# A spectral filter and a gated FFN on one core: four excursions per batch moved to other steps, their output buffers to another pool, and the last block's copies to VectorE

## The chip, the core and the metric

The kernel runs on one core of a Trainium2 chip. The metric is the device time of one execution in microseconds (us). Times inside an execution come from one profiled execution, counted from the start of its span. Engines: PE is TensorE (PEld its weight loads), DVE is VectorE, ACT is ScalarE, POOL is GpSimd, SP is SyncE, which here issues nearly all DMAs.

## The reference

The input x is 8 x 3008 x 256 (batch, sequence, channel). Along the sequence each channel is multiplied in the frequency domain by a filter; the result, as 24064 tokens of 256 channels, goes through a gated FFN with 1536 hidden units.

```python
X = np.fft.rfft(x, axis=1)
Y = X * (filt_r + 1j * filt_i)[None]
y = np.fft.irfft(Y, n=3008, axis=1).reshape(24064, 256)
out = (np.maximum(y @ w_gate, 0) * (y @ w_val)) @ w_out
```

## The kernel before

The sequence length is split as 3008 = 94 x 32, and the transform is done in stages by matmuls. For a batch b:

- **Stage A** (transforms of length 94) reads x and writes the buffer Abuf[b] in device memory.
- **Stage B** reads it back into the tile `at`, does the transforms of length 32, multiplies by the filter and transforms back; it writes Dbuf[b]. It has 14 items (`items_b`), most with two psX matmuls, two multiplications on DVE, four psD matmuls and a copy on ACT (dsb). Four of the items end with a store to Dbuf.
- **Stage C** (`item_c`) reads Dbuf[b] back into dC tiles and forms one half of the FFN's input tile yT, 512 tokens wide.
- **The FFN** goes over 47 blocks of 512 tokens. A block has 12 steps. In each step `gv` does four matmuls (psV, psG) for 128 hidden units, ACT copies psV to vsb and DVE forms prod from psG and vsb; `o_part` does four psO matmuls of the block before. At steps 5 and 11 of a block, psO is copied to osb and stored to the output. Steps are numbered through: step s is step s mod 12 of block s // 12.

Batch 0, and batch 1's stage A, are done in a prologue in a form of their own (`items_a`), in which ACT copies to the tile `asb` and SP stores it to Abuf. The other stages are woven into the FFN's steps: a table `side` says which functions are called at which step, after that step's gv and o_part. The engines work in the order in which the program was written, each with its own queue; semaphores connect them. Nothing is rescheduled.

For batches 2 to 7 stage A is done in four chunks j. Three calls belong to a chunk:

- `load_chunk`: six DMAs on SP from x to the tile XP[j % 2]. There are two such tiles, so chunk 2 uses that of chunk 0 again, and chunk 3 that of chunk 1.
- `fold_chunk`: six additions and subtractions on POOL, in XP and a second tile, `fold`.
- `tiled_a`, the excursion: 16 matmuls in the source (32 records in the trace) on quarters of the array, 24 rows by 32 columns, from XP and `fold` to four PSUM tiles psF; four copies to bf16 in the tile `asf`, two on ACT and two on DVE; four DMAs on SP from asf to Abuf.

Then `load_at_tiled` reads Abuf back with eight DMAs. The first item of stage B stands at step sb0: 93, 165, 237, 309, 381 and 453 for batches 2 to 7. The items stand at sb0, sb0 + 2, ..., sb0 + 26, all odd steps; batch 1's begin at 19. At sb0 + 27 `load_d` asks SP for the eight reads of Dbuf. [...]

Memory on the chip comes from pools. `sb` lasts for the whole kernel, `pro` is closed after the prologue, and `fs` is opened then, in the memory that pro had. A tile of fs has to wait for whatever still uses the tiles of pro that were there. Before the change asb lies in pro, and asf in fs.

In the last block `o_part` runs alone after all gv; its four copies are on ACT, of 128x256 each, and part of the stores is issued by ACT too.

Of the kernel before, what the change touches and what calls it, by code (L numbers as in the profile page):

```python
# [13 lines left out]
BF16 = mybir.dt.bfloat16  # L14
# [16 lines left out]
NROW = 96  # L31
# [4 lines left out]
def _ap(t, offset_elems, ap_list):  # L36
    return dataclasses.replace(
        t, offset=t.offset + offset_elems, ap=[list(p) for p in ap_list]
    )
# [82 lines left out]
def kernel(  # L122
# [10 lines left out]
    nc = tc.nc  # L133
    B, S_, D = x.shape
    DFF = moe_w_gate.shape[1]
    NFT = DFF // 128
    assert S_ == S and D == 256 and DFF % 128 == 0
    NC2 = 8
# [11 lines left out]
    sb = ctx.enter_context(tc.tile_pool(name="sb", bufs=2))  # L150
    ps = ctx.enter_context(tc.tile_pool(name="ps", bufs=2, space=bass.MemoryType.PSUM))
    prologue = ExitStack()
    pro = prologue.enter_context(tc.tile_pool(name="pro", bufs=1))
# [110 lines left out]
    def fft_tag():  # L264
        turn["i"] += 1
        return turn["tags"][turn["i"] % len(turn["tags"])]

    def items_a(b):

        def one(c, j, st):  # L270
            if j == 0:
                st["asb"] = pro.tile([NROW, NC2 * D], BF16, tag="asb", bufs=4, name="asb")
            psA = ps.tile([128, 512], FP32, tag=fft_tag(), name="psA")
            o = (c * NC2 % NX2) * D + j * 512
            nc.tensor.matmul(psA[0:NROW], WA[:, :NROW], XF[c * NC2 // NX2][:, o:o + 512],  # L275
                             start=True, stop=True)
            dst = st["asb"][:, j * 512:(j + 1) * 512]
            nc.scalar.copy(dst, psA[0:NROW])
            if j == 3:
                nc.sync.dma_start(_ap(Abuf[b], c * NROW * NC2 * D, [[NC2 * D, NROW], [1, NC2 * D]]),  # L280
                                  st["asb"])
        for c in range(N2 // NC2):
            st = {}
            for j in range(NC2 * D // 512):
                yield lambda c=c, j=j, st=st: one(c, j, st)
# [3 lines left out]
    def load_chunk(b, j):  # L289

        xp = XP[j % 2]
        for q in range(4):
            r, o = 32 * q, 8 * q + 2 * j
            nc.sync.dma_start(xp[r:r + 24, 0:4:2, :],
                              _ap(x, (b * N1 * N2 + o) * D,
                                  [[N2 * D, 24], [47 * N2 * D, 2], [1, 512]]))
        for i in range(2):
            nc.sync.dma_start(xp[:, 2 * i + 1, :],
                              _ap(x, ((b * N1 + 46 + 47 * i) * N2 + 2 * j) * D,
                                  [[8 * D, 4], [-N2 * D, 32], [1, 512]]))  # L300

    def fold_chunk(b, j):

        xp = XP[j % 2]
        t = fs.tile([128, 2, 512], FP32, tag="fold", bufs=2, name="fold")
        tt = nc.gpsimd.tensor_tensor
        tt(t, xp[:, 0:2], xp[:, 2:4], op=ALU.add)  # L307
        tt(xp[:, 2:4], xp[:, 0:2], xp[:, 2:4], op=ALU.subtract)  # L308
        tt(xp[:, 0], t[:, 0], t[:, 1], op=ALU.add)
        tt(t[:, 0], t[:, 0], t[:, 1], op=ALU.subtract)  # L310
        tt(t[:, 1], xp[:, 2], xp[:, 3], op=ALU.add)
        tt(xp[:, 2], xp[:, 2], xp[:, 3], op=ALU.subtract)
        fold[b, j] = (xp[:, 0], t[:, 0], t[:, 1], xp[:, 2])

    def tiled_a(b, j):

        banks = [ps.tile([128, 2, D], FP32, tag=t, name="psF") for t in ("psv", "psg", "fft", "fft")]
        for q in range(4):
            r = 32 * q
            for c in range(4):  # L320
                nc.tensor.matmul(banks[q][32 * c:32 * c + 32], WF[r:r + 24, c, :],  # L321
                                 fold[b, j][c][r:r + 24], start=True, stop=True,
                                 tile_position=(r, 32 * c))
        asf = fs.tile([128, 2, 4, D], BF16, tag="asf", bufs=2, name="asf")
        for q in range(4):
            copy = nc.scalar.copy if q % 2 == 0 else nc.vector.tensor_copy
            copy(asf[:, :, q, :], banks[q])  # L327
        for c in range(4):
            nc.sync.dma_start(_ap(Abuf[b], ((48 * (c % 2) + 24 * (1 - c // 2)) * N2 + 8 * j) * D,
                                  [[N2 * D, 24], [1, 8 * D]]),  # L330
                              asf[32 * c:32 * c + 24])

    def load_at_tiled(b):

        ats[b] = sb.tile([128, NG, D], BF16, tag="at", bufs=1, name="at")
        for rr in range(4):
            for e in range(2):
                nc.sync.dma_start(ats[b][32 * rr:32 * rr + 32, e:NG:2, :],
                                  _ap(Abuf[b], (48 * (rr % 2) + 24 * e + 12 * (rr // 2)) * N2 * D,
                                      [[D, 32], [N2 * D, 12], [1, D]]))  # L340
# [5 lines left out]
    def load_at(b, c):  # L346
        if c == 0:
            ats[b] = sb.tile([128, NG, D], BF16, tag="at", bufs=1, name="at")
        nc.sync.dma_start(ats[b][c:c + 125:4],
                          _ap(Abuf[b], c * NROW * NC2 * D, [[D, 32], [4 * NC2 * D, NG], [1, D]]))  # L350
# [52 lines left out]
    def load_d(b, z0=0, z1=NZ):  # L403
        for z in range(z0, z1):
            dC = sb.tile([NROW, 4, D], BF16, tag="dC", bufs=12)
            nc.sync.dma_start(dC, _ap(Dbuf[b], z * 4 * NROW * D,
                                      [[D, NROW], [NROW * D, 4], [1, D]]))
            dCs[b, z] = dC
# [3 lines left out]
    def runs(t, n):  # L412

        o = 0
        while o < n:
            b, r = divmod(t + o, S)
            n2, n1 = divmod(r, N1)
            w = min(N1 - n1, n - o)
            yield o, b, n2, n1, w
            o += w  # L420
# [34 lines left out]
    def o_part(blk, s, prods):  # L455

        t = s // 3
        last = blk == NB - 1
        if s in (0, 6) or last and s in (3, 9):
            ost["ps"] = ps.tile([128, 2, D], FP32, tag="psv" if s in (3, 9) else "pso", name="psO")  # L460
        psO = ost["ps"]
        for ft in range((s % 3) * 4, (s % 3) * 4 + 4):
            nc.tensor.matmul(psO[:, t % 2], prods[ft][:, t * 128:(t + 1) * 128], WoT[:, ft, :],  # L463
                             start=(ft == 0), stop=(ft == NFT - 1))
        if s in (5, 11) or last and s % 3 == 2:
            t0 = t if last else t - 1
            osb = fs.tile([128, 2, D], FP32, tag="osb", bufs=5)
            nc.scalar.copy(osb[:, t0 % 2:t % 2 + 1], psO[:, t0 % 2:t % 2 + 1])  # L468
            for tt in range(t0, t + 1):
                for i, (o, b, n2, n1, w) in enumerate(runs(blk * W + tt * 128, 128)):  # L470

                    cut = w // 16 * 16 if last else 0
                    for c0, c1 in ((0, cut), (cut, w)):
                        if c0 < c1:
                            eng = nc.scalar if last and (t + i) % 2 else nc.sync
                            eng.dma_start(_ap(out, (b * S + (n1 + c0) * N2 + n2) * D,
                                              [[N2 * D, c1 - c0], [1, D]]),
                                          osb[o + c0:o + c1, tt % 2])
# [11 lines left out]
    q = NX2 * D // 4  # L490
# [65 lines left out]
    fs = ctx.enter_context(tc.tile_pool(name="fs", bufs=2))  # L556
# [10 lines left out]
    def at_step(s, f):  # L567
        side.setdefault(s, []).append(f)
# [5 lines left out]
    for b in range(1, B):  # L574
        end = (b * S // W - 1) * NFT + C_AT[0] - 5
        sb0 = 19 if b == 1 else end - 30 | 1
        if b == 1:
            for c in range(4):
                at_step(5, lambda c=c: load_at(1, c))
        else:  # L580
            for j in range(4):
                e = sb0 - 16 - NFT * (3 - j)
                at_step(e - 23, lambda b=b, j=j: load_chunk(b, j))
                at_step(e - 22, lambda b=b, j=j: fold_chunk(b, j))
                at_step(e, lambda b=b, j=j: tiled_a(b, j))
            at_step(e + 4, lambda b=b: load_at_tiled(b))
        for i, f in enumerate(items_b(b)):
            at_step(sb0 + 2 * i, f)
        at_step(sb0 + 27, lambda b=b: load_d(b))
    prev = None  # L590
    for k in range(NB):
        prods = []
        for ft in range(NFT):
            gv(k, ft, prods)
            if prev is not None:
                o_part(prev[0], ft, prev[1])
            for f in side.get(k * NFT + ft, ()):
                f()
            if ft in C_AT and k + 1 < NB:
                item_c(k + 1, C_AT.index(ft))  # L600
        prev = (k, prods)
# [30 lines left out]
```

## Time and profile before

| | us |
|---|---|
| three runs | 926.00, 926.95, 928.22; median 926.95 |
| profiled execution | 927.01 |
| its span, first to last instruction | 925.2 |
| PE busy | 897.4 (97%) |
| DVE, ACT, POOL busy | 576.8, 505.3, 260.6 |
| mean granted PE clock | 0.991 |

The prologue ends at about 62 us, when the first gv starts. From 100 us on PE is busy for nearly all the time. A share of busy time says nothing on which wait matters where; the chain of waits and the timelines do.

### The profile page before, as it was taken

To read this page: it belongs to the slowest core of one execution; us is meant where nothing else is said; L and a number is where in the kernel's file an instruction comes from. 1 tells how busy PE (TensorE), PEld (TensorE's weight loads), DVE (VectorE), ACT (ScalarE), POOL (GpSimd) and SP (SyncE) were. 2 spreads that over 40 slices of the span, in tenths; PEclk is the share of its full clock that TensorE was granted. 3 is DMA by queue.
4 is the path that set the end of the run, shared out by engine and by line. 5 is a ranking of instruction groups with operands and counts; after the bars stand their busy time and mean duration, and the time that the engine had idled before them with its cause. 6 is when DMAs were issued, how large, how long until landed. Compare 5 with 4: busy or idle time off the path is not lost.

```text
span 925.2 us, 17992 instructions
## 1 busy us (share of the span) xinstructions
PE 897.4 (97%) x6488; PEld 546.7 (59%) x6602; DVE 576.8 (62%) x871; ACT 505.3 (55%) x897; POOL 260.6 (28%) x180
## 2 busy tenths in 40 slices
PE   8779999999999999999999999999999999999997
PEld 3435665566655665556655566655665566666665
DVE  3716865568655686557755577555875568655552
ACT  4655555555555555555555555555555555555553
POOL 4320444404444054322543125440444400000000
PEclk9899999999999999999999999999999999999999
DMA  9996345353453533553344533535335252231111
GB/s 253 257 249 131 104 129 146 89 128 104 126 150 88 128 104 116 155 118 86 108 146 137 114 105 111 153 100 124 99 120 170 64 118 64 63 102 36 35 30 50
DMA packets 106138, 109.04 MB, mean 118 GB/s; under 512 B 9794, under 2 KB 87362, under 8 KB 105410
## 3 DMA queue, kind: packets, MB, share of 16 engines
q1 hardware_dynamic: 101222, 103.77, 40.4%
q0 software_dynamic: 4512, 3.90, 2.7%
q8 instruction: 52, 0.85, 0.4%
q14 instruction: 36, 0.29, 0.1%
q10 hardware_dynamic: 316, 0.22, 0.1%
HBM read 61.94 MB, written 49.81 MB: 121 GB/s over the span
## 4 chain that ended last, share of the span: by engine, by line
PE 90%; DMA 4%; ACT 2%; DVE 2%; issue 1%; SPq 0%; POOL 0%; ACTq 0%; POOLq 0%
PE psG L444 26%; PE psO L463 25%; PE psV L444 24%; PE psF L321 4%; PE psA L275 3%; PE psD L383 2%; PE psD L382 2%; PE psX L363 2%; PE psY L428 2%; DVE prod L449 2%; ACT vsb L447 1%; DMA XF<-in_x_dram 1%; DMA Dbuf<-dsb 1%; DMA Abuf<-asb 1%; DMA out_dram<-osb 1%
## 5 line engine op out<-in xcount | busy, mean ns | idle before, releaser
L449 DVE SCALAR_TENSOR_TENSOR prod<-psG,vsb 128x512 bf16<-128x512 f32 x564 | 389.9, 692 | 288.5 <-ACT vsb L447 277.8
L447 ACT CAST vsb<-psV 128x512 bf16<-128x512 f32 x564 | 331.5, 588 | 270.2 <-PE psV L444 159.4
L463 PE MATMUL psO<-WoT,prod 128*128 128x256 bf16 x2256 | 336.6, 273 | 1.3
L444 PE MATMUL psG<-yT,WgT 128*128 128x512 bf16 x1102 | 331.1, 380 | 4.0
L444 PE MATMUL psV<-yT,WvT 128*128 128x512 bf16 x1041 | 318.7, 381 | 6.8 <-ACT vsb L447 4.5
L463 PEld LDWEIGHTS <-prod 128*128 128x128 bf16 x2256 | 220.6, 98 | 143.5
L444 PEld LDWEIGHTS <-WgT 128*128 128x128 bf16 x1128 | 110.3, 98 | 134.8 <-issue 2.2
L307 POOL TENSOR_TENSOR fold<-XP 128x1024 f32<-128x1024 f32 x24 | 56.4, 2348 | 416.0 <-DMA out_dram<-osb 151.4
L444 PEld LDWEIGHTS <-WvT 128*128 128x128 bf16 x1128 | 102.5, 98 | 38.5 <-issue 26.8
L385 ACT CAST dsb<-psD 128x512 bf16<-128x512 f32 x96 | 55.9, 587 | 51.8 <-PE psD L383 50.1
L468 ACT COPY osb<-psO 128x512 f32<-128x512 f32 (+1 forms) x96 | 55.3, 577 | 31.9 <-PE psO L463 24.5
L366 DVE TENSOR_TENSOR tt<-psX,Ftr 128x512 bf16<-128x512 f32 x96 | 65.2, 681 | 4.3 <-PE psX L363 4.3
L372 DVE TENSOR_TENSOR uu<-psX,Fti 128x512 bf16<-128x512 f32 x90 | 61.3, 681 | 0.0
L308 POOL TENSOR_TENSOR XP<-XP 128x1024 f32<-128x1024 f32 x24 | 56.4, 2350 | 1.9
L383 PE MATMUL psD<-uu,I2u 128*128 128x256 bf16 x192 | 47.7, 276 | 0.6 <-POOL uu L370 0.6
L382 PE MATMUL psD<-tt,I2t 128*128 128x256 bf16 x192 | 47.9, 276 | 0.0
L327 DVE CAST asf<-psF 128x512 bf16<-128x512 f32 x48 | 31.5, 687 | 16.6 <-PE psF L321 15.9
L363 PE MATMUL psX<-at,F 128*128 128x256 bf16 x192 | 37.8, 281 | 4.1 <-DMA at<-Abuf 4.1
L433 ACT CAST yT<-psY 128x512 bf16<-128x512 f32 x47 | 27.5, 585 | 24.0 <-PE psY L428 23.9
L435 DVE CAST yT<-psY 128x512 bf16<-128x512 f32 x47 | 32.0, 681 | 12.9 <-PE psY L428 12.9
L428 PE MATMUL psY<-M,dC 96*128 96x94 bf16 (+18 forms) x604 | 37.7, 199 | 1.1 <-DMA dC<-Dbuf 1.1
L321 PE MATMUL psF<-XP,WF 24*32 24x512 f32 x384 | 37.1, 597 | 0.0
(63 smaller groups left out, 437.9 us busy)
## 6 DMA issues: line engine op xcount, KB each, us to landing
dC<-Dbuf SPq DMA_DIRECT2D x64, 192.0 KB
XP<-in_x_dram SPq DMA_DIRECT2D x48, 256.0 KB
Dbuf<-dsb SPq DMA_DIRECT2D x31, 384.0 KB
XP<-in_x_dram SPq DMA_DIRECT2D x96, 96.0 KB
Abuf<-asf SPq DMA_DIRECT2D x96, 96.0 KB
at<-Abuf SPq DMA_DIRECT2D x48, 192.0 KB
out_dram<-osb SPq DMA_DIRECT2D x70, 94.0 KB
XF<-in_x_dram SPq DMA_DIRECT2D x12, 256.0 KB
```

Source lines behind the costliest of these rows:

```text
L307: tt(t, xp[:, 0:2], xp[:, 2:4], op=ALU.add)
L308: tt(xp[:, 2:4], xp[:, 0:2], xp[:, 2:4], op=ALU.subtract)
L321: nc.tensor.matmul(banks[q][32 * c:32 * c + 32], WF[r:r + 24, c, :], fold[b, j][c][r:r + 24], start=True, stop=True, tile_position=(r, 32 ...
L363: nc.tensor.matmul(psX[:, i], F2[:, g + i, :], at[:, g + i, :], start=True, stop=True)
L366: nc.vector.tensor_tensor(tt, psX, Ftr[:, g:g + 2, :], op=ALU.mult)
L372: nc.vector.tensor_tensor(uu, psX, Fti[:, g:g + 2, :], op=ALU.mult)
L382: nc.tensor.matmul(psD[:, i], I2t[:, g + i, :], tt[:, i], start=True, stop=False)
L383: nc.tensor.matmul(psD[:, i], I2u[:, g + i, :], uu[:, i], start=False, stop=True)
L444: nc.tensor.matmul(pt[:, :W], w[:, h, ft * 128:(ft + 1) * 128], yt[:, h, :], start=(h == 0), stop=(h == 1))
L447: nc.scalar.copy(vsb, psV[:, :W])
L449: nc.vector.scalar_tensor_tensor(prod, in0=psG[:, :W], scalar=0.0, in1=vsb, op0=ALU.max, op1=ALU.mult)
L463: nc.tensor.matmul(psO[:, t % 2], prods[ft][:, t * 128:(t + 1) * 128], WoT[:, ft, :], start=(ft == 0), stop=(ft == NFT - 1))
```

## The change

The tile of A's output is now `asb` of the pool sb in both forms of stage A, with four buffers (128 x 2048 in bf16, of which the prologue's form uses 96 rows). The four excursions of a batch, which were 12 steps apart with load and fold 23 and 22 steps ahead of each, are now at sb0 - 41, - 33, - 27 and - 17, with the loads at sb0 - 66, - 60, - 40 and - 32. Before they were at sb0 - 52, - 40, - 28 and - 16; the first of these was a step that also has an item of the batch before's stage B. In the last block DVE copies psO to osb instead of ACT.

```diff
@@ items_a
-                st["asb"] = pro.tile([NROW, NC2 * D], BF16, tag="asb", bufs=4, name="asb")
+                st["asb"] = sb.tile([128, NC2 * D], BF16, tag="asb", bufs=4, name="asb")
...
@@ tiled_a
-        asf = fs.tile([128, 2, 4, D], BF16, tag="asf", bufs=2, name="asf")
+        asf = sb.tile([128, NC2 * D], BF16, tag="asb", bufs=4, name="asb")
+        asf = asf.rearrange("p (n q d) -> p n q d", n=2, d=D)
@@ o_part
-            nc.scalar.copy(osb[:, t0 % 2:t % 2 + 1], psO[:, t0 % 2:t % 2 + 1])
+            copy = nc.vector.tensor_copy if last else nc.scalar.copy
+            copy(osb[:, t0 % 2:t % 2 + 1], psO[:, t0 % 2:t % 2 + 1])
@@ the table of steps
-            for j in range(4):
-                e = sb0 - 16 - NFT * (3 - j)
-                at_step(e - 23, lambda b=b, j=j: load_chunk(b, j))
-                at_step(e - 22, lambda b=b, j=j: fold_chunk(b, j))
-                at_step(e, lambda b=b, j=j: tiled_a(b, j))
-            at_step(e + 4, lambda b=b: load_at_tiled(b))
+            for j, (l, e) in enumerate(((-66, -41), (-60, -33), (-40, -27), (-32, -17))):
+                at_step(sb0 + l, lambda b=b, j=j: load_chunk(b, j))
+                at_step(sb0 + l + 1, lambda b=b, j=j: fold_chunk(b, j))
+                at_step(sb0 + e, lambda b=b, j=j: tiled_a(b, j))
+            at_step(sb0 + e + 4, lambda b=b: load_at_tiled(b))
```

More of the change, by code (lines that the diff above doesn't have):

```diff
@@ L276, in one @@
                              start=True, stop=True)
-            dst = st["asb"][:, j * 512:(j + 1) * 512]
+            dst = st["asb"][:NROW, j * 512:(j + 1) * 512]
             nc.scalar.copy(dst, psA[0:NROW])
@@ L280, in one @@
                 nc.sync.dma_start(_ap(Abuf[b], c * NROW * NC2 * D, [[NC2 * D, NROW], [1, NC2 * D]]),
-                                  st["asb"])
+                                  st["asb"][:NROW])
         for c in range(N2 // NC2):
```

## Prediction

> **What bounds the kernel now.** I read the page's busy shares first, then TensorE's waits, the chain of work in order of time, and for one batch the timelines of SP and GpSimd.
>
> ```profile
> PE 897.4 (97%) x6488; PEld 546.7 (59%) x6602; DVE 576.8 (62%) x871; ACT 505.3 (55%) x897; POOL 260.6 (28%) x180
> PE psV L444 <- ACT vsb L447: 4.5, 1, 4.5
> PE psY L428 <- DMA dC<-Dbuf: 1.1, 1, 1.1
> ```
>
> TensorE is the bound: from 100 to 850 us it is busy for 98 to 99% of every stretch, so whatever keeps it waiting is added to the time in full, and a saving on another engine counts only where TensorE waits for it. In the whole FFN stage it has two waits of over 1 us: 4.5 us for the first vsb copy, and 1.1 us once for a dC read.
>
> ```profile
> 63.90:66.00 2.10, 0.02 (x1) 0.00 (x0) 0.00 (x0) 0.00 (x0) 0.00 (x0) 0.99 1.20 291
> 66.00:68.40 2.40, 0.00 (x0) 0.00 (x0) 0.00 (x0) 0.62 (x2) 0.71 (x1) 0.50 1.24 246
> 68.40:72.80 4.40, 4.38 (x11) 1.62 (x11) 2.67 (x4) 1.63 (x3) 2.84 (x2) 0.50 1.28 231
> ```
>
> These stretches surround that 4.5 us wait (columns: stretch, length, busy time of PE, PEld, DVE, ACT, POOL, then granted clock, DMA share, GB/s). The idle time is followed by 4.4 us at half clock.
>
> ```profile
> 237.30 2.13 PE psF L321 x32
> 257.14 1.26 PE psF L321 x32
> 274.62 1.26 PE psF L321 x32
> 292.05 1.26 PE psF L321 x32
> ```
>
> The chain shows batch 3's four A excursions (start, length). The first stands at a step that also has an item of stage B, and takes 2.13 instead of 1.26 us. All six batches show this pattern.
>
> ```profile
> 237.30 1.70 SPq L476 DMA_DIRECT2D out_dram<-osb  x5
> 239.09 1.39 SPq L387 DMA_DIRECT2D Dbuf<-dsb  x1
> 240.59 1.96 SPq L329 DMA_DIRECT2D Abuf<-asf  x4
> 242.64 1.98 SPq L294 DMA_DIRECT2D XP<-in_x_dram  x4
> 252.64 0.35 SPq L387 DMA_DIRECT2D Dbuf<-dsb  x1
> 259.29 3.98 SPq L406 DMA_DIRECT2D dC<-Dbuf  x8
> 263.37 1.60 SPq L476 DMA_DIRECT2D out_dram<-osb  x4
> 265.32 2.64 SPq L329 DMA_DIRECT2D Abuf<-asf  x4
> 268.33 2.01 SPq L294 DMA_DIRECT2D XP<-in_x_dram  x4
> 254.76 2.35 POOL L307 TENSOR_TENSOR fold<-XP 128x1024 f32<-128x1024 f32 x1 [12.18 <-DMA XP<-in_x_dram]
> 263.66 1.27 POOL L312 TENSOR_TENSOR XP<-XP 128x512 f32<-128x512 f32 x1
> 280.43 2.35 POOL L307 TENSOR_TENSOR fold<-XP 128x1024 f32<-128x1024 f32 x1 [15.51 <-DMA out_dram<-osb]
> 289.32 1.27 POOL L312 TENSOR_TENSOR XP<-XP 128x512 f32<-128x512 f32 x1
> ```
>
> This decides the case: SP issues the load of chunk 2 at 242.64, GpSimd starts its fold at 254.76 and ends it at 264.93; chunk 3: 268.33, 280.43, 290.59. So load to folded takes 22.3 us here; over the twelve loads of chunks 2 and 3 I find 20.3 to 22.7, mean 21.4. It is 10.2 us of fold, the rest transfer. In the kernel before, chunk 2 is due 24 steps after chunk 0 (237.23 to 274.56), and waits for nothing.
>
> [...] idle 29.4 to 33.5 and 63.9 to 68.4 us, clock 0.5 from 31.8 to 38.7 and from 66.0 to 72.8. [...] SP stands from 252.99 to 259.29 at the first dC read until D has landed, and everything behind it is late. [...]
>
> **The change, part by part.** A step is 1.30 us (psG starts at 258.77 and 260.07), 1.36 more with an A excursion (psO ends 256.98, next psV 258.33), about 0.25 more with an item C.
>
> *1. A's output buffers leave the prologue's pool.* In the built program the first vsb copy (ScalarE), the first prod (VectorE) and the XP memset (GpSimd) wait, before, for the last four Abuf<-asb stores, since their memory was asb's; these waits are gone after. The next latest of the remaining releasers is the last psA matmul (60.9 us). So the third gv's psV starts at 62.89+0.87=63.8 instead of 68.42: 4.6 us, and the half clock of 68.4 to 72.8 doesn't come: 2.2 more. **-6.8** (ends 4.5, if dC reads or weights are now late, and 6.9). As for the four buffers that the excursions now share: the A stores land before the next use, cost nothing.
>
> *2. No collision with stage B.* 6 x (2.13-1.26) = **-5.2**. By the built program the excursions of batch 3 stand at steps 124, 132, 138, 148, where B has 93 to 119 and 165 on, odd ones. I take 1.26 at the new places; bounds 1.15 and 1.40, the trace's extremes.
>
> *3. The same moves shorten a lead.* Every excursion has its load (6 DMAs on SP), fold (6 operations on GpSimd) and 4 Abuf stores on SP. Leads from load to excursion: 25, 27, 13, 15 steps, instead of 23. XP has two buffers, so the load of chunk 2 stands behind excursion 0 in any case, and is now due 14 steps after it:
> - Time there is: 14 x 1.30 + 2 x 0.25 (C at 128, 130) + 2 x 1.36 (excursions 0, 1) = 21.4 us.
> - Time it needs: d + 21.4, d being the time from excursion 0's first matmul to the load on SP. So **TensorE waits d** at excursion 2 of each batch, with all later FFN steps behind it in its queue.
> - d in the kernel before is 4.9 to 6.2 for chunk 2 (237.23 to 242.64), 9.2 to 12.5 for chunk 3 (257.07 to 268.33), where the eight dC reads are ahead on SP. After, these reads (step 120) come just ahead of excursion 0 (step 124). In batch 3's clock: the last D store is issued near 251.2 (five out stores from 249.55), as no XP load is ahead of it; it lands in 4 to 5 us (A stores of 294.63 release the at load at 298.76: 4.1), so dC issues near 255.8. From the dC reads to the load, with the same DMAs between, it was 9.0, 10.5 and 10.6 in batches 3 to 5. So the load comes near 265.6, excursion 0 at 257.07-1.30=255.8: d = 9.8. In batch 2 the reads stand two steps further ahead: some 7.5. Sum 5 x 9.8 + 7.5 = **+56.5**, with ends 6 x 5.4 = 32 (no reads in the way) and 6 x 13.5 = 81 (D lands as late as before, dC at 259.3).
> - Each such idle stretch exceeds the 4.1 and 4.5 us that gave half clock. What ran at half clock after those was 5.1 and 4.4 us, so 2.4 us lost: 6 x 2.4 = **+14.4**.
> - Chunk 3: behind a load SP stands until it has landed (the out stores from 271.68 take 9.84 us, to 281.5, and that load's fold began at 280.43), so chunk 3's load starts when chunk 2's fold does, and its own fold ends some 22 us later, 12 after the end of chunk 2's. Excursion 3 comes 14.9 us after excursion 2. Free, with 3 us in hand. Chunks 0 and 1 have 25 steps or more. The at load keeps 13 steps to B instead of 12.
>
> *4. dC.* They are issued some 3.5 us earlier, so the one psY wait goes: **-1.1** (0 to -1.1).
>
> *5. Last block's copies on VectorE.* On ScalarE the third and fourth stand behind its own DMA issues: 920.47 and 921.73, though TensorE ends at 919.4. VectorE is free from 914.7; its 128x256 f32 copy isn't shown, half of its 128x512 (0.69) gives 0.35, as ScalarE's 0.37. But the DMA issues themselves wait for earlier ones; I take **-0.6** (0 to -2).
>
> Sum: -6.8-5.2-1.1-0.6+56.5+14.4 = +57.2. The profiled execution took 927.01 (span 925.2 and 1.8 around it), like the median of 926.95: **984 us**.
>
> **Rivals.** (a) *The load isn't late*: SP issues it at once and the fold is ready in time; then only the gains are left, 927.0-13.7 = 913 us. It decides if excursion 0 to fold end is 21.4 us or less; the trace has 26.2 to 28.0 in all six batches even without dC reads between, against it. 4%. (b) *Short waits*: dC reads don't delay the load, d = 5.4: +32+14-14 gives 960. 15%. (c) *Long waits*: D lands late and excursion 3 waits too: +81+14-14, some 1008. 13%. (d) The main case, d of 8 to 11: 973 to 995. 68%.
>
> **How the numbers follow.** Likeliest 984. The range takes in (b) and most of the way to (c): 955 to 1004. A change under 0.2% can't be told from none here; faster is (a) alone, 0.04; same 0.01; slower 0.95.
>
> **What would show it.** After: a PE wait of psF (weight load or matmul) on GpSimd's fold at excursion 2 of each batch, six times 7 to 11 us, and none at 0, 1, 3; PEclk down at six places; the 4.5 us vsb wait gone, psF 1.26 everywhere at full clock. No such six waits, or a time under 950, would prove the main step wrong.

## The result and the profile after

The change makes the kernel slower: 985.18 us (four runs, 982.14 to 986.96) against 926.48 us for the kernel before on the same chip, a ratio of 1.063 (95% interval 1.059 to 1.066). The profiled execution took 984.0 us, its span is 982.2 against 925.2 before. The forecast was 984.

From the page of the kernel after, TensorE's and the other engines' busy time, and the granted clock in 40 slices:

```profile
PE 926.8 (94%) x6489; PEld 551.7 (56%) x6602; DVE 578.0 (59%) x875; ACT 501.1 (51%) x893; POOL 260.2 (26%) x180
...
PEclk9999998999979999799997999979999799999999
```

As many matmuls as before take 29 us more, though the share of busy time has fallen from 97 to 94%. Nearly 25 us of them are psF's, which is busy for 61.7 us where it was for 37.1, since excursion 2 is now stretched out, as the next views show; the rest is in other matmuls, which in part run at half clock. The clock row shows where, at six places of nearly equal distance, one for each of batches 2 to 7.

The waits, of the matmuls and then of the weight loads (engine, tile and line that wait, what for, sum, times, longest):

```profile
PE psF L321 <- POOL XP L309: 30.6, 6, 6.3
PE psX L364 <- DMA at<-Abuf: 4.9, 1, 4.9
```

```profile
PEld psF L321 <- POOL XP L309: 32.3, 6, 6.6
...
PEld psF L321 <- POOL fold L310: 7.1, 6, 1.2
PEld psF L321 <- POOL fold L311: 7.0, 6, 1.2
PEld psF L321 <- POOL XP L312: 7.0, 6, 1.2
```

Six waits of psF for GpSimd's fold are new; the 4.5 us wait for vsb and the 1.1 us wait for dC are gone. The three shorter groups show that TensorE starts the excursion as soon as the third of the fold's six results is there (L309), and then gets the last three at GpSimd's pace, one each 1.34 us. So the wait of 30.6 us is not the whole stall, and the sign that the forecast named, six waits of 7 to 11 us, is not in this list as it was put: the six are 5.1 us on the mean. Counted to the end of the fold they are 7.2 to 10.3.

The chain of work that ended last, batch 3 (start, length, what):

```profile
255.76 1.26 PE psF L321 x32
...
265.43 4.26 DMA XP<-in_x_dram
269.71 3.02 SPq L478
273.61 3.64 DMA Abuf<-asb
277.37 2.34 POOL fold L307
279.77 2.35 POOL XP L308
282.19 1.27 POOL XP L309
283.50 6.33 PE psF L321 x32
```

Excursion 0 takes 1.26 us, no longer 2.13. Excursion 2 takes 6.33, not the 1.26 that the forecast had everywhere, and ahead of it the chain leaves TensorE for the load and the fold. One label misleads: the fold at L307 reads XP and not Abuf. By the semaphore events the second of chunk 2's two L298 loads lands at 277.15, within 0.1 us of the end that the chain gives to an A store (273.61 + 3.64); it is the load that the fold waits for.

SP's timeline in the same batch (these rows answer to those from 249.55 on before), and from GpSimd's the first and the last fold operation of chunk 2:

```profile
249.47 1.80 SPq L478 DMA_DIRECT2D out_dram<-osb  x5
251.37 0.35 SPq L388 DMA_DIRECT2D Dbuf<-dsb  x1
256.35 4.64 SPq L407 DMA_DIRECT2D dC<-Dbuf  x8
261.09 1.64 SPq L330 DMA_DIRECT2D Abuf<-asb  x4
263.01 2.32 SPq L478 DMA_DIRECT2D out_dram<-osb  x4
265.43 1.57 SPq L294 DMA_DIRECT2D XP<-in_x_dram  x4
267.21 1.14 SPq L298 DMA_DIRECT2D XP<-in_x_dram  x2
268.83 4.66 SPq L478 DMA_DIRECT2D out_dram<-osb  x5
273.61 4.50 SPq L330 DMA_DIRECT2D Abuf<-asb  x4
279.19 1.56 SPq L294 DMA_DIRECT2D XP<-in_x_dram  x4
```

```profile
277.35 2.34 POOL L307 TENSOR_TENSOR fold<-XP 128x1024 f32<-128x1024 f32 x1 [32.10 <-DMA Abuf<-asb]
...
286.20 1.26 POOL L312 TENSOR_TENSOR XP<-XP 128x512 f32<-128x512 f32 x1
```

This is the forecast's step 3 nearly to the number. The dC reads leave SP at 256.35, when D has landed, the load follows 9.1 us later at 265.43, and the fold ends 22.0 us after that. From excursion 0's first matmul to the load it is 9.74 us (forecast 9.8). Over the six batches this d is 6.95, 9.74, 11.04, 9.30, 9.25 and 8.99, and from excursion 0 to the end of chunk 2's fold it is 28.56, 31.77, 31.59, 31.32, 30.61 and 29.73 us, where the steps in between give 21.4. Chunk 3's load starts at 279.19, 1.8 us after chunk 2's fold has begun, and excursion 3 waits in no batch: its fold is ready 4.0 to 7.2 us ahead.

Two sets of stretches, one at the first vsb copies and one across excursion 2 of batch 3 (stretch, length, busy time of PE, PEld, DVE, ACT, POOL, granted clock, DMA share, GB/s):

```profile
60.00:63.00 3.00, 2.31 (x18) 1.10 (x18) 0.69 (x1) 1.84 (x4) 1.59 (x1) 1.00 1.09 313
63.00:66.00 3.00, 2.95 (x15) 1.36 (x14) 1.96 (x3) 2.09 (x4) 1.95 (x2) 1.00 1.17 289
66.00:69.00 3.00, 3.00 (x16) 1.34 (x14) 2.31 (x5) 2.01 (x4) 0.00 (x0) 1.00 1.24 249
279.00:281.00 2.00, 0.00 (x0) 0.00 (x0) 0.00 (x0) 0.00 (x0) 1.92 (x2) 1.00 0.40 124
281.00:283.00 2.00, 0.00 (x0) 0.00 (x0) 0.00 (x0) 0.00 (x0) 1.92 (x2) 0.86 0.50 124
283.00:285.00 2.00, 1.50 (x3) 0.34 (x4) 0.00 (x0) 0.00 (x0) 1.84 (x3) 0.50 0.35 89
285.00:287.00 2.00, 2.00 (x4) 0.19 (x3) 0.00 (x0) 0.00 (x0) 1.92 (x2) 0.50 0.25 84
287.00:289.50 2.50, 2.50 (x28) 0.58 (x26) 0.00 (x0) 0.03 (x1) 0.47 (x1) 0.50 0.28 104
289.50:292.70 3.20, 2.98 (x20) 1.34 (x10) 1.98 (x3) 1.62 (x3) 2.20 (x1) 0.50 0.36 101
292.70:296.00 3.30, 3.30 (x26) 2.02 (x25) 1.36 (x2) 1.70 (x4) 3.14 (x3) 1.00 0.23 71
```

At 63 to 69 us, where TensorE stood and then ran at half clock before, it is busy at full clock. At 279 to 283 it stands. Look at 285 to 287: four matmul records fill "busy 2.00", since they overlap and their ends are modelled. That is a TensorE that is fed one result at a time, not one at work. Then 5.2 us after the fold's end are still at half clock, and over the six batches 3.6 to 6.7 us, 32.1 in all.

### The profile page after: what moved, and what is told of

Same layout as the page of the kernel before. It is cut to its first block, busy times and chain, and to the rows that moved or that the text cites. A ratio compares the mean times of both kernels' runs of the same rounds, so it can differ in the third digit from the quotient of the medians.

```text
span 982.2 us, 17960 instructions
## 1 busy us (share of the span) xinstructions
PE 926.8 (94%) x6489; PEld 551.7 (56%) x6602; DVE 578.0 (59%) x875; ACT 501.1 (51%) x893; POOL 260.2 (26%) x180
## 4 chain that ended last, share of the span: by engine, by line
PE 85%; DMA 6%; POOL 4%; DVE 2%; ACT 1%; SPq 1%; issue 1%; ACTq 0%; POOLq 0%
PE psG L445 23%; PE psO L464 23%; PE psV L445 22%; PE psF L321 6%; PE psA L275 3%; PE psD L384 2%; PE psD L383 2%; PE psX L364 2%; PE psY L429 2%; DMA Abuf<-asb 2%; POOL XP L308 1%; POOL fold L307 1%; DVE prod L450 1%; DMA out_dram<-osb 1%; DMA XF<-in_x_dram 1%; ACT vsb L448 1%
## 5 line engine op out<-in xcount | busy, mean ns | idle before, releaser
L450 DVE SCALAR_TENSOR_TENSOR prod<-psG,vsb 128x512 bf16<-128x512 f32 x564 | 390.1, 692 | 285.0 <-ACT vsb L448 268.9
L307 POOL TENSOR_TENSOR fold<-XP 128x1024 f32<-128x1024 f32 x24 | 56.3, 2346 | 477.4 <-DMA out_dram<-osb 160.3
L321 PE MATMUL psF<-XP,WF 24*32 24x512 f32 x384 | 48.2, 706 | 30.6 <-POOL XP L309 30.6
L328 DVE CAST asb<-psF 128x512 bf16<-128x512 f32 x48 | 30.9, 686 | 77.2 <-PE psF L321 64.5
L328 ACT CAST asb<-psF 128x512 bf16<-128x512 f32 x48 | 25.8, 589 | 92.1 <-PE psF L321 92.1
L470 ACT COPY osb<-psO 128x512 f32<-128x512 f32 x92 | 53.9, 585 | 22.7 <-PE psO L464 20.4
L321 PE MATMUL psF<-fold,WF 24*32 24x512 f32 x384 | 53.7, 712 | 0.3 <-POOL fold L310 0.3
```

What stands on the lines that cost most here:

```text
L450: nc.vector.scalar_tensor_tensor(prod, in0=psG[:, :W], scalar=0.0, in1=vsb, op0=ALU.max, op1=ALU.mult)
```

## The experiments

Each ratio is to the kernel before on the same chip, where its median was 926.0 to 926.8 us.

### The gains without the new spacing

The edit puts the old lines of the table of steps back and keeps the rest of the change.

```diff
-            for j, (l, e) in enumerate(((-66, -41), (-60, -33), (-40, -27), (-32, -17))):
...
+            for j in range(4):
+                e = sb0 - 16 - NFT * (3 - j)
+                at_step(e - 23, lambda b=b, j=j: load_chunk(b, j))
...
```

> The steps of the excursions are those of the kernel before; the pool of A's output and the last block's copies are those of after. Theory: without the schedule no wait of psF on the fold exists; the 4.5 us wait for the first vsb and the half clock behind it are gone, 6.8 us, and the tail gains some 0.3: 920 (919 to 921), psF still 2.13 us at six places. Rival: the wait passes to the next of the many releasers of the closed pool, and the time is that of before, 926 to 927.

Measured: 919.61 us (918.94 to 920.20), ratio 0.992 (0.990 to 0.994). The 4.5 us wait for vsb is gone from the list of waits. So the pool and the copies are a gain of some 7 us, and the whole loss lies in the spacing.

### The old spacing, moved by one step

Excursion 0 stands at sb0 - 53, off stage B's item; the others are as before. The edit is shown against the kernel above.

```diff
-                e = sb0 - 16 - NFT * (3 - j)
+                e = sb0 - 16 - NFT * (3 - j) - (j == 0)
```

> After, with the excursions 12 steps apart again and the leads of before (load 23 steps, fold 22 steps ahead), and only excursion 0 moved, from sb0-52 to sb0-53, a step without an item of stage B. Two buffers of XP. Theory: the collision alone cost 0.9 us a batch, and 25 steps between excursions 0 and 2 are enough for load and fold: 914 (912.5 to 916), psF 1.26 everywhere, the same time as with the third buffer. Rival: the step between two items of B is as bad as one with an item, since it shares the PSUM buffers with the next item: 919 to 920, as with the pools alone.

Measured: 915.81 us (914.36 to 917.39), ratio 0.989 (0.987 to 0.990). No psF wait is left, and every step with an excursion takes 2.66 us, those of excursion 0 as well. Taking the collision away needs no other spacing: one step is enough.

### Excursion 2 six steps later

```diff
-((-66, -41), (-60, -33), (-40, -27), (-32, -17))
+((-66, -41), (-60, -33), (-40, -21), (-32, -17))
```

> After, with excursion 2 at sb0-21 instead of sb0-27. It is due 8.3 us later, where the fold was 7 to 10 us late. Theory: the wait at excursion 2 falls to 0 to 2 us, but chunk 3's load stands behind chunk 2's on the same engines, and its fold ends 10.6 to 13.5 us after chunk 2's, while excursion 3 is now due 6.6 us after excursion 2; so the wait moves to excursion 3, 4 to 7 us each, with its half clock: 965 (955 to 972). Rival: chunk 3 is independent, and the wait simply goes: 914 to 920.

Measured: 969.05 us (967.70 to 970.22), ratio 1.046 (1.044 to 1.048). TensorE's wait at the third result is down to four times and 7.8 us:

```profile
PE psF L321 <- POOL XP L309: 7.8, 4, 2.8
```

That the wait would move on is what was expected: the steps of excursion 3 now take 7.6 to 10.7 us instead of 2.66, in all six batches. Six steps are 7.8 us; the steps of excursion 2 have become 8.4 to 9.2 us shorter, half clock included, and the next one in the chain of buffers, which had 4 to 7 us in hand, is late.

### A third buffer

Three XP tiles and three fold tiles, so that chunk 2's load waits for no excursion of its batch; loads of chunks 2 and 3 at sb0 - 56 and sb0 - 40. To make room, osb has four buffers instead of five and prod 22 instead of 24.

```diff
-        xp = XP[j % 2]
+        xp = XP[(4 * b + j) % 3]
...
-((-66, -41), (-60, -33), (-40, -27), (-32, -17))
+((-66, -41), (-60, -33), (-56, -27), (-40, -17))
```

> After, with three XP and three fold buffers (one osb and two prod buffers fewer, to make room), the load of chunk 2 moved from sb0-40 to sb0-56 and that of chunk 3 from sb0-32 to sb0-40; the excursions stand where after has them. Theory: the load of chunk 2 no longer stands behind excursion 0, no psF waits for a fold, and only the gains are left: 914 (912 to 917), psF 1.26 everywhere, clock as before. Rival: something else in the new places of the excursions costs, as the PSUM buffers or the copies; then waits of TensorE stay at the excursions, and the time is over 930.

Measured: 913.53 us (913.13 to 913.76), ratio 0.985 (0.984 to 0.987): the fastest kernel of this study. The excursions stand at the steps of the change and psF waits nowhere. So the steps of the excursions themselves cost nothing; what costs is that chunk 2's load comes only after excursion 0, where two XP tiles hold it. The run does two things at once, the third tile and the load 16 steps sooner. A third tile with the load left at sb0 - 40 was not run. In the kernel after, excursion 0 has ended by 257.0 us, and it is SP's other work that holds the load until 265.43; so a third tile without the earlier load may not help. The forecast's gains, -13.7 us, are what is left: 927.0 - 13.7 = 913.3.

### The half clock

Filler matmuls of 512 columns ahead of excursion 2 give TensorE work in its wait; their result goes to a PSUM tile that nothing reads. First 28, then 40 of them.

```diff
+    def filler(n):
+        psJ = ps.tile([128, 512], FP32, tag="fft", name="psJ")
+        for i in range(n):
+            nc.tensor.matmul(psJ, WvT[:, 0, 0:128], WvT[:, 0, 0:512], start=True, stop=True)
...
+                if j == 2:
+                    at_step(sb0 + e, lambda: filler(28))
```

> After, with 28 matmuls of 512 columns on the FFN's weights (their result is not used) ahead of excursion 2 of each batch: 6.0 us of TensorE work at full clock, put into a wait of 7 to 10 us. Theory: the fold still ends when it did, so the work itself costs nothing, and [...] the half clock mostly does not come: some 16 us less, 969 (966 to 975), mean clock over 0.98. Rival: the half clock costs nothing of its own, since TensorE waits there anyway: 984 to 986, or 1021 if the fold does not bound and the 6 x 6.0 us are added.

Measured with 28: 982.26 us (981.88 to 982.73), ratio 1.060 (1.058 to 1.062): a miss. The wait up to the start of excursion 2 is filled, but for 0.9 us in batch 5 and 0.1 in batch 4, and yet the half clock came in five of six batches. TensorE's timeline in batch 3 shows what lies between the fillers and the rest of the excursion:

```profile
278.71 2.75 PE L338 MATMUL psJ<-WvT 128*128 128x512 bf16 x12
281.40 1.04 PE L321 MATMUL psF<-XP,WF 24*32 24x512 f32 x2
282.27 1.04 PE L321 MATMUL psF<-fold,WF 24*32 24x512 f32 x2
283.61 1.04 PE L321 MATMUL psF<-fold,WF 24*32 24x512 f32 x2 [0.30 <-POOL fold L311]
284.95 0.69 PE L321 MATMUL psF<-XP,WF 24*32 24x512 f32 x2 [0.30 <-POOL XP L312]
```

For 3.5 us only six small matmuls start, as GpSimd ends its last operations. The clock falls at 286.5. Why so little was gained can be counted: at half clock are 27.3 us of the FFN stage, no longer 64.9, but most of what went had stood in the wait, where it cost nothing. After the fold's end it is 24.3 us, where it was 32.1, and half of the difference is 3.9 us; 2.9 were measured.

> As the filler of 28 matmuls, but 40 of them (8.6 us), since with 28 the half clock still came in five batches, from inside the last 4 us, in which excursion 2 stands started and waits for the fold's last three results. After's waits to the end of the fold were 7.2, 10.3, 10.1, 9.9, 9.0 and 8.3 us, so 0 to 1.7 are left, and 1.4 is added in batch 2. Theory: [...] the clock stays full from 40 us on, and of after's 16 us lost at half clock all but 2 or 3 come back: 971 (968 to 975). Rival: the half clock is no loss of its own: 982 to 985.

Measured with 40: 972.85 us (971.5 to 975.13), ratio 1.051 (1.049 to 1.052), the mean clock 0.993 instead of 0.963. In batch 3 the fillers end near 285.0 and 1.4 us of the trickle are left, with no half clock; of the six stretches at half clock one remains, in batch 5, where 1.5 us of it are left. So the half clock costs at least 985.2 - 972.9 = 12.3 us: it is a loss apart from the stall. The count agrees: after the fold's end 3.4 us at half clock are left of 32.1, half of the difference is 14.3, and the fillers take back 1.4 us in batch 2 and 0.6 in batch 7, where they run past the fold's end.

### What makes chunk 2's load late

Five runs take away one candidate or two. The first lets GpSimd issue the dC reads, so that SP need not stand until D has landed. The second reads a quarter of dC's bytes and issues them as before. The third does both.

```diff
-            nc.sync.dma_start(dC, _ap(Dbuf[b], z * 4 * NROW * D,
+            eng.dma_start(dC, _ap(Dbuf[b], z * 4 * NROW * D,
...
-        at_step(sb0 + 27, lambda b=b: load_d(b))
+        at_step(sb0 + 27, lambda b=b: load_d(b, eng=nc.gpsimd))
```

```diff
+            if b:
+                nc.sync.dma_start(dC[:, 0], _ap(Dbuf[b], z * 4 * NROW * D, [[D, NROW], [1, D]]))
+                dCs[b, z] = dC
+                continue
...
```

> After, with the eight dC reads of each batch (behind stage B) issued by GpSimd instead of SP. Theory: SP no longer stands at the wait for D to land, so the load of chunk 2 is issued some 6 us after excursion 0 instead of 9.2 on the mean (7.0 in batch 2, 9.0 to 11.0 in the others); load to fold end stays 20.5 to 22; five waits shrink by 3 to 4 us each: 967 (960 to 974). Rival: the load is late because the DMA engines are busy with the dC data, whoever issues it; then load to fold end grows or nothing changes, 983 to 987.

> After, with each dC read of batches 1 to 7 cut to a quarter of its bytes (one row of the four is read, and stage C uses it for all four); as many DMAs on SP, with the same waits. It leaves out three quarters of D's reads. With the reads on GpSimd the load was issued 1 to 4 us earlier after excursion 0, but landed no earlier (21.5 us after excursion 0's first matmul in batch 3, as in after), so what stands ahead on the DMA engines may decide, and not SP's order. Theory of the data: load to landing and the waits for earlier DMAs on SP shrink, excursion 0 to fold end goes from 31.3 to 28: 968 (962 to 975). Theory of SP's order: the wait for D's landing and eight issues stay, excursion 0 to fold end is 30 to 31: 978 to 984.

> After, with both edits on dC together: GpSimd issues the reads, and each reads a quarter of its bytes (one row of four, used for all four; the other three quarters are left out of the computation's input). Theory 'two causes that cover each other' (SP's stand at the dC reads and the dC bytes in the engines; each alone is replaced by the other): excursion 0 to fold end comes down to 27 to 28.5, waits 4 us shorter each, near 968 (962 to 973). Rival 'something else sets it' (the out stores, A stores and the narrow XP loads): as with the quarter reads alone, 976 to 982.

The fourth writes each of the two 256 KB loads of a chunk as four loads of 32 rows. The same number of bytes is read, but the rows of a group run forward and no longer backward, so the mirrored half gets other data; the run changes the shape and the direction together. The last adds the first edit to it.

```diff
-            nc.sync.dma_start(xp[:, 2 * i + 1, :],
-                              _ap(x, ((b * N1 + 46 + 47 * i) * N2 + 2 * j) * D,
-                                  [[8 * D, 4], [-N2 * D, 32], [1, 512]]))
+            for q in range(4):
+                nc.sync.dma_start(xp[32 * q:32 * q + 32, 2 * i + 1, :],
+                                  _ap(x, ((b * N1 + 15 + 47 * i) * N2 + 2 * j + 8 * q) * D,
+                                      [[N2 * D, 32], [1, 512]]))
```

> After, with each of the two 256 KB loads of a chunk (L298, four groups of 32 rows) written as four loads of one group of 32 rows[...]; same bytes, but the rows are read in forward order instead of mirrored, so the input of the mirrored half is other data. It tells apart why excursion 2's load lands late. The DMA share of after is 0.25 in 270-272 and 276-278 us, while nothing but these two loads runs. Theory 'narrow loads' (the two loads run on a quarter of the engines and one after the other, at 70 to 83 GB/s): load to fold end falls from 21.4 by some 4 us, the six waits by 4 us each, 985 - 24 = 961 (955 to 970). Rival 'issues' (SP's order decides; six more DMAs per chunk to issue at some 0.5 us each, the transfers were not the limit): no gain or some loss, 982 to 990.

> The wide loads, with the dC reads issued by GpSimd as well. If the narrow loads set the landing, taking SP's stand at the dC read away now counts, d some 2 us less: 950 to 960. If SP's issues are the limit, the six more DMAs cost and this gives them back: 978 to 986. If the dC bytes in the engines are the limit, it is like the wide loads alone.

Measured, each as the mean over the six batches, in us from excursion 0's first matmul:

| kernel | first load's issue starts (d) | last load's issue ends | last load landed | fold ends | median of the runs (ratio, interval) |
|---|---|---|---|---|---|
| after | 9.21 | 12.26 | 20.27 | 30.60 | 985.18 (1.063, 1.059 to 1.066) |
| dC reads on GpSimd | 7.25 | 12.41 | 20.88 | 31.21 | 988.11 (1.066, 1.064 to 1.068) |
| a quarter of dC | 7.55 | 10.89 | 19.28 | 29.62 | 977.77 (1.056, 1.054 to 1.057) |
| both | 6.40 | 10.65 | 18.66 | 29.00 | 972.81 (1.050, 1.048 to 1.053) |
| wide loads | 9.18 | 15.46 | 17.26 | 27.68 | 969.89 (1.047, 1.044 to 1.051) |
| wide loads, dC on GpSimd | 7.42 | 16.52 | 18.40 | 28.81 | 972.28 (1.049, 1.046 to 1.052) |

The fold's end puts the six kernels in the same order as the medians do, and six times its difference gives the difference in time to within 3 us: wide loads 6 x (27.68 - 30.60) = -17.5, measured -15.3.

*dC on GpSimd* was a miss. SP no longer stands and d is 2 us shorter, but the six loads are then issued over 5.2 us instead of 3.1, and the last lands 0.6 us later than before. In the kernel after SP's DMAs use eight semaphores in turn, and some issues come right upon the landing of the DMA eight ahead: the last three of the four out stores of 263.01 are issued at 263.82, 264.48 and 265.01, and the dC reads eight ahead land at 263.81, 264.46 and 265.00. So SP was paced there by what was in flight, and not only by the wait for D. The reads' bytes have not gone either: GpSimd's queue moves 1.57 MB of them from 260 to 270 us in batch 3, around the first load's issue at 263.75.

*A quarter of dC* lands between the two forecasts and decides neither alone. *Both* come to 972.81, 12 us under after: the two causes do cover each other in part. But the 27 to 28.5 us that the theory of two causes gave are not reached (28.2 to 29.6), and 968 is not either; the time lies within the range that it had, at the edge.

*Wide loads* give the most, at the edge of their range: from the first load's issue to the end of the fold it is 18.5 us instead of 21.4, 2.9 us less where some 4 had been expected. d is the same, and the issue of the last load ends 3.2 us later. The time from that issue to the landing falls from 8.0 to 1.8 us. In one stretch of the kernel after nothing but the L298 loads of chunk 2 moves, an instruction fetch that ends at 272.41 apart; the number before the last is the DMA share:

```profile
272.00:273.00 1.00, 1.00 (x8) 0.56 (x6) 0.49 (x1) 0.52 (x1) 0.00 (x0) 1.00 0.26 100
```

The share is 0.26, and the two loads land at 274.43 and 277.15, 2.7 us apart. That such a load runs on a quarter of the engines is the author's reading of this share; the runs show what four loads in its place gain, and not why. Of the stretches that the expectation names, 270-272 holds an instruction fetch beside the loads, and in 276-278 out stores and A stores make up most of the 0.25. Whether the backward rows had a part in the slow loads was not tested apart. With wide loads, SP and GpSimd in the same batch:

```profile
264.83 1.57 SPq L294 DMA_DIRECT2D XP<-in_x_dram  x4
266.46 4.42 SPq L299 DMA_DIRECT2D XP<-in_x_dram  x8
```

```profile
272.77 2.35 POOL L308 TENSOR_TENSOR fold<-XP 128x1024 f32<-128x1024 f32 x1 [33.09 <-PE psG L446]
```

The fold starts 7.9 us after the first load's issue, where it was 11.9. In the list of waits:

```profile
PE psF L322 <- POOL XP L310: 13.2, 6, 3.2
```

It was 30.6. With dC on GpSimd as well, the time is not shorter (the intervals overlap), as in the pair without wide loads. Of the three forecasts for it that is the one for dC's bytes; the 950 to 960 us did not come. Why the twelve loads then take 9.1 us to issue instead of 6.3 was not taken apart further.

## Why the prediction was right

The difference of the two spans is 982.2 - 925.2 = 57.0 us; the forecast was +57.2. By its steps, from the start times of the FFN steps in both traces:

| step of the forecast | forecast | measured |
|---|---|---|
| 1. vsb no longer waits, no half clock there | -6.8 | -6.8 |
| 2. no collision with stage B | -5.2 | -5.3 |
| 3. TensorE waits for chunk 2 | +56.5 | +54.8 |
| 3. half clock after it | +14.4 | +15.2 |
| 4. dC earlier | -1.1 | -1.2 |
| 5. copies of the last block | -0.6 | -0.25 |
| prologue, not in the forecast | 0 | +0.4 |
| sum | +57.2 | +56.9 |

- *Step 1* was right in both of its parts, and the kernel with the pools and copies alone, 919.61, shows it apart from the rest.
- *Step 2* was right; the old spacing with excursion 0 one step off shows it with the steps of 2.66 us. In the medians, taken on two chips, it is less than 5.2 us: 919.61 to 915.81. At the new places an excursion takes 1.26 us as well.
- *Step 3, the stall*: the time that there is (21.4) was worked out from the steps, the time that it needs from d and the transfers. The measured waits from the due time to the end of the fold are 7.2, 10.3, 10.1, 9.9, 9.0 and 8.3, sum 54.8; the forecast had 7.5 for batch 2 and 9.8 for the others. The third buffer and the moved old spacing show that this is the cause: with chunk 2's load ahead of excursion 0, or with 25 steps between excursions 0 and 2, the wait is gone.
- *Step 3, the half clock*: its size was right, the picture behind it too simple. The forecast let TensorE stand until the fold had ended. It starts at the third result, and trickles. In the run with 28 fillers, which fill the wait itself but for 0.9 and 0.1 us, the half clock came in five of six batches all the same, with this trickle. In the two stretches of the forecast the clock fell 2.4 us (29.4 to 31.8) and 2.1 us (63.9 to 66.0) after TensorE had stopped. In the kernel after the six falls came 2.1 to 5.2 us after the last matmul ahead of the wait. That 2.4 us of loss for each stall, taken from these two stretches alone, met the measured mean of 2.5 is in part luck, as the batches differ: they have 3.6 to 6.7 us at half clock after the fold's end, of which half is lost.
- *Step 3, chunk 3*: free, as forecast, but not far from its limit, as the run with excursion 2 later shows.
- *Step 5* was mis-sized. The four DVE copies take 0.42 us each (the forecast had 0.35) and follow psO at once, but the stores behind them are what ends the kernel. DVE's last copy, and ACT's issues:

```profile
976.68 0.42 DVE L470 COPY osb<-psO 128x256 f32<-128x256 f32 x1 [0.89 <-PE psO L464]
```

```profile
973.20 6.18 ACTq L478 DMA_DIRECT2D out_dram<-osb  x9
```

ACT is still issuing at 979.4, 2.3 us after the last copy, and SP until 980.2. The forecast's DMA issues that wait for earlier ones show in both traces: before, ACT's issues at 919.13 and 920.06 came 0.02 us after landings of earlier out stores, at 919.11 and 920.04; after, those at 976.36, 977.12 and 978.12 did, with landings at 976.34, 977.10 and 978.10.

Where the forecast's reasoning was weaker than its number: rival (b) took "d = 5.4" to mean a time of 960, with the 21.4 us from load to folded as a constant. It isn't one. In the run with both edits on dC, d is 6.4 and the time from load to folded is 22.6 us; with dC on GpSimd alone it is 24.0. The sum of d and 21.4 held in the kernel after since the DMAs around the load were the same ones as before, in the same order. And the forecast gave d to SP's stand at the dC read; SP's stand, dC's bytes and the narrow loads each have a part, and the narrow loads have the largest that a single edit took away. That part lies inside the 21.4, which was measured before and not taken apart.

## What to carry to other kernels

When a step is moved, take its lead in time from each thing that it needs and compare it with the time that this needs, above all where a buffer ties it to another step that is moved too: here excursion 2 went from 24 to 14 steps after excursion 0, with its load still to come between the two, and a gain of 13 us became a loss of 57. Where a wait falls on TensorE, price the clock that comes with it as well; here it was 15 us on 55. To find what delays a load, follow the landing and not the issue: a shorter wait on the issuing queue brought nothing by itself, with the narrow loads or with the wide ones (985 to 988 us, 970 to 972), and it did bring 5 us once the dC reads had a quarter of their bytes (978 to 973).

## What the runs showed of the hardware that was not expected

- In the traces of the kernels before and after, each stretch at half clock (the end of the execution left out) lasted 3.41 us or two, three or four times that: after, 3.41 us in the prologue and 6.83, 10.24, 13.65, 13.65, 10.24 and 10.24 us in batches 2 to 7; before, 6.83 us twice. The six falls of the kernel after lay 119.47, 119.47, 122.88, 122.88 and 122.88 us apart, 35 or 36 times 3.413, and the 3.41 us ahead of a fall held up to 1.4 us of full-size matmuls. How far this sets what a stall costs was not shown.
- With 28 fillers only six small matmuls, two at a time and up to 1.3 us apart, started in the last 2.4 to 4.0 us of the fold in batches 3 to 7, and the clock fell in all five, as in batch 3 at 286.5, where TensorE is busy for 1.40 of the 2 us from 283 to 285 by the profile; in batch 2 this stretch was 1.4 us, and it did not fall. With 40 fillers it was 0 to 1.5 us, and the clock fell in one of six, where it was 1.5.
- In the kernel after, the second 256 KB load of a chunk (four groups of 32 rows) landed 2.5 to 3.0 us after the first, in all 24 chunks; written as four loads of 32 rows each, all eight pieces of chunk 2 in batch 3 landed within 2.2 us (270.19 to 272.39), though they took 4.4 us to issue.
- In the kernel after, two issues on SP came with the landing of the DMA eight ahead, though they do not need what that one brings: the A stores at 274.45 and 277.16 come within 0.02 us of the landing of chunk 2's two L298 loads, at 274.43 and 277.15.
